# Loading w_tok in two halves, loading w_ch1 later, and a new order of the opening and the weave, in a block-sparse attention followed by a ResMLP block

## The chip, the core and the metric

The kernel runs on one core of one Trainium2 chip. That core has five engines that run side by side, each with an instruction stream of its own: PE (matrix multiply and transposes), DVE (vector), ACT (activation functions), POOL (GpSimd, elementwise work and the issue of loads) and SP (issue of transfers). Each stream is executed in order, so an instruction that waits holds up everything behind it on its engine. The metric is device microseconds (us) of one execution; lower is better.

## What is computed

```
scores = q @ k^T / 8, masked in blocks of 32 (neighbours, first and last
         block, and 3 sampled blocks a row); attn = softmax(scores)
x   = attn @ v                 # 4 batches, 8 heads of 64, 768 tokens
a1  = alpha1 * x + beta1       # heads side by side: 512 columns
u   = x + lam * (w_tok @ a1)   # w_tok: 768 x 768, mixes tokens
a2  = alpha2 * u + beta2
out = u + lam * (relu(a2 @ w_ch1) @ w_ch2)   # 512 -> 2048 -> 512
```

All inputs are float32; the work is done in bfloat16 and float16, with sums in float32.

## The kernel before

**Pairs and units.** Heads are worked in pairs: 16 pairs (4 batches of 4), pair i with heads w = 0 and 1. A pair's scores are cut into nine units, each of which is one `emit_qk` (PE, L583), one `emit_exp` (ACT, L601) and, two units later, its `emit_pv` (PE, L630 or L653), which multiplies by v and by a column of ones. When a head is complete, `emit_finish` divides on DVE (L670, L671) into x_sb, and `emit_a1pp` makes `a1pp`, the affine input of the token mixing, in two instructions (L687, L688), on POOL or, where `A1V` holds 1 (index 2i + w) or a batch ends, on DVE. `job_tok` then multiplies by the transposed w_tok (L795, six matmuls a block of 128 tokens), or, for the later pairs, `job_tok2` (L819, 12 matmuls a token T below). The result is added to x_sb and cast (L810 or L831, L837), transposed into `uT` (by PE, L846, or by a DMA, `emit_udma` and `emit_uscale`), and fed to the MLP: `job_f1` (four matmuls L884, relu L891 on ACT) and `job_f2` (L903, four matmuls a call, then an add L912 and a store).

**Two score buffers.** QK of unit u writes one of two `sp` buffers in PSUM and must wait until exp of unit u - 2 has read it.

**The opening** (the loop over `s`, 45 steps, pairs 0 to 4). Step s issues QK(s), exp(s), the jobs that `PLAN` gives it with a fraction under 0.5, PV of unit s - 2, and then the jobs with a fraction of 0.5 or more. A slot in `PLAN` is that step number. Step 2, 11, 20 and so on also issue loads that no slot has asked for yet. From step 42 (`OPEN`), `POUR[s - 42]` calls of `job_f1` come in between. In the opening the mask is part of the score (24 extra rows in `kText` and `qText`); `rows1` to `rows3` copy these rows on DVE or POOL (L439), `layv00` and `layv01` cast pair 0's v (L313), `layk01` and `layq01` cast the second head's k and q, and `tps0` transposes them and copies them out of PSUM (L471). QK(4) is the first unit that reads the second head. `bcast0` to `bcast2` spread lam, alpha1 and beta1 over the partitions (L719, L728, L730), `lv1` and so on copy a pair's v (L313), `tk` and `tq` transpose a pair's k and q on PE (L493), `mask0` to `mask17` build the mask for the later pairs on POOL (L519), `lam0` to `lam16` scale w_ch2 by lam on DVE (L765).

**Loads.** `emit_load` (L302), `emit_wtk_load` (L772), `emit_w1_load` (L753) and `emit_w2_load` (L759) are issued by POOL and share one DMA queue. The raw k and v of a pair each have two buffers, so a load waits for the copy or transposes that read the buffer two pairs ago. w_tok is one load of all its tokens; its six jobs `wt0` to `wt5` (`emit_wtok_t`) each transpose one of six interleaved columns for all 768 output tokens (six transposes, one copy), so `tok` of any block needs all six.

**The weave** (from pair 5 on) is an order written out by hand: one string for three units, `W1` for pairs 5 to 7, `W2` for 8 to 11 and again for 12 to 15, `W3` for the rest. `q` issues the three QK and the first exp, `x` a further exp, `k` the multiplication of an exp by the mask (DVE, L618), `p` the PV of one key block, `f` and `g` one call of `job_f1` and `job_f2`, `T` one `job_tok2`, `s` opens a finished pair's jobs, `d` and `v` its `emit_udma` and `emit_uscale`, `L` a load, `Q`, `K` and `Y` the next pair's q, k (DMA transposes issued by SP) and v, and `0`, `1`, `2` the slots of `PLAN` from 45 on.

**PSUM.** Besides the two `sp` buffers there are three `mm` buffers for everything else and one `op` for PV.

Of the kernel before, what the change touches and what calls it, by code (L numbers as in the profile page):

```python
# [13 lines left out]
BF = mybir.dt.bfloat16  # L14
# [6 lines left out]
S = 768  # L21
# [5 lines left out]
P = 128  # L27
NT = S // P
# [9 lines left out]
OPEN = 42  # L38
UTD = [1, 1]
TDM = [1, 0]  # L40
A1V = [1, 0, 0, 1, 0, 0, 0, 1]
POUR = [3, 1, 1]
W1 = [
# [9 lines left out]
]  # L53
W2 = [
# [12 lines left out]
]  # L67
W3 = [
# [3 lines left out]
]  # L72
WEAVE = W1 + W2 * (B - 2) + W3
ENG = {
# [16 lines left out]
    "tq1": 0,  # L91
}
PLAN = {
    "layv00": 0.29,
    "wtkl": 0.42,
    "warm1": 0.49,
    "loadv2": 0.58,
    "layk01": 1.22,
    "layq01": 1.25,
    "mask_cols": 1.5,  # L100
    "rows1": 2.08,
    "tps0": 2.52,
    "parts": 2.83,
    "mask1": 2.94,
    "w1_0": 2.96,
    "tq1": 4.55,
    "layv01": 4.3,
    "rows2": 4.5,
    "tk1": 4.82,
    "lv1": 5.01,  # L110
    "bcast0": 5.1,
    "rows3": 5.84,
    "loadk3": 6.08,
    "bcast2": 6.12,
    "loadv3": 7.02,
    "mask3": 7.41,
    "loadk2": 8.21,
    "loadq2": 8.52,
    "bcast1": 8.8,
    "loadq3": 9.23,  # L120
    "a1pp0": 9.37,
    "w1_2": 9.64,
    "w1_1": 10.3,
    "columns": 11.32,
    "wt2": 11.35,
    "wt1": 11.76,
    "wt5": 12.19,
    "lv2": 12.84,
    "wt4": 13.01,
    "wt0": 13.43,  # L130
    "loadv4": 13.94,
    "w1_3": 14.3,
    "tq2": 14.44,
    "loadq4": 14.54,
    "wt3": 15.31,
    "columns_use": 16.32,
    "tk2": 16.6,
    "tok0_0": 17.05,
    "tok0_1": 17.4,
    "tk3": 18.13,  # L140
    "loadk4": 18.23,
    "tok0_2": 20.0,
    "tq3": 20.4,
    "mask8": 20.72,
    "loadk5": 20.73,
    "mask2": 20.89,
    "tok0_3": 21.32,
    "tok0_4": 22.02,
    "lv3": 22.91,
    "mask6": 22.94,  # L150
    "mask0": 23.62,
    "tok0_5": 23.87,
    "loadq5": 24.3,
    "tok1_0": 24.53,
    "mask4": 24.64,
    "w2_0": 24.82,
    "mask7": 25.08,
    "lv4": 25.4,
    "tok1_1": 25.6,
    "tok1_2": 27.2,  # L160
    "loadv5": 27.53,
    "tok1_3": 27.74,
    "tok1_4": 28.91,
    "tok1_5": 29.7,
    "w2_2": 29.98,
    "mask5": 30.09,
    "tq4": 30.41,
    "mask15": 30.72,
    "udma0": 30.82,
    "tk4": 31.72,  # L170
    "udma1": 31.9,
    "w2_1": 32.02,
    "tq5": 32.51,
    "mask9": 32.65,
    "tok2_0": 33.91,
    "tk5": 34.64,
    "usc0": 34.69,
    "tok2_1": 34.88,
    "mask14": 34.9,
    "mask13": 35.48,  # L180
    "tok2_2": 35.71,
    "mask11": 35.79,
    "tok2_3": 36.37,
    "lam16": 37.24,
    "mask17": 37.68,
    "w2_3": 37.7,
    "mask16": 37.75,
    "tok2_4": 37.77,
    "mask10": 37.9,
    "tok3a_0": 38.34,  # L190
    "tok3a_1": 38.43,
    "tok2_5": 38.51,
    "tok3a_2": 38.52,
    "tok3a_3": 38.85,
    "tok3a_4": 39.48,
    "tok3b_0": 39.51,
    "tok3b_1": 39.52,
    "tok3b_2": 39.53,
    "tok3b_3": 39.54,
    "ut2": 39.85,  # L200
    "tok3a_5": 40.02,
    "mask12": 40.23,
    "tok3b_4": 40.23,
    "usc1": 40.28,
    "lv5": 40.42,
    "ut3_0": 40.8,
    "tok3b_5": 41.21,
    "cast3": 42.22,
    "lam2": 42.25,
    "lam3": 43.09,  # L210
    "ut3_1": 43.63,
    "lam1": 44.85,
    "lam10": 44.92,
    "lam9": 45.25,
    "lam7": 45.27,
    "lam0": 45.32,
    "lam11": 45.58,
    "lam6": 45.9,
    "lam13": 46.09,
    "lam5": 47.61,  # L220
    "lam14": 47.82,
    "lam4": 47.9,
    "lam8": 49.72,
    "lam12": 49.8,
    "lam15": 50.13,
}


# [1 line left out]
def kernel(  # L230
# [16 lines left out]
    nc = tc.nc  # L247
# [30 lines left out]
    def ptile(shape, dt, name):  # L278
        return pp.tile(shape, dt, name=name, tag=name)
# [44 lines left out]
    identb = const[:, 0:P]  # L324
# [65 lines left out]
    for o in (slice(0, 4), slice(4, NT)):  # L390
# [4 lines left out]
        out=eqt,  # L395
# [55 lines left out]
    def mm_tile(shape=(P, DM), dt=FP):  # L451
        return psum.tile(list(shape), dt, name="mm", tag="mm", bufs=3)
# [210 lines left out]
    def emit_finish(i, w):  # L663
        b, hp = i // NP, i % NP
        if (hp, w) == (0, 0):
            x_sbs[b] = ap_.tile([P, NT, DM], FP, name="x_sb", tag="x_sb", bufs=3)
        op, n = ops.pop((i, w))
        assert n == 36
        rcp = ap_.tile([P, NT], FP, name="rcp", tag="rcp", bufs=2)
        nc.vector.reciprocal(out=rcp[:], in_=op[:, :, D])  # L670
        nc.vector.tensor_tensor(  # L671
            out=x_sbs[b][:, :, ts(2 * hp + w, D)],
            in0=op[:, :, 0:D],
            in1=rcp[:].unsqueeze(2).broadcast_to([P, NT, D]),
            op=ALU.mult,
        )
# [20 lines left out]
    wtokT = ptile([P, NT, S], BF, "wtokT")  # L697
# [5 lines left out]
    parts = ptile([P, P], BF, "parts")  # L703
# [63 lines left out]
    wtks = {}  # L767

    def emit_wtk_load():
        t = ap_.tile([P, NH, QC], BF, name="hts", tag="hts", bufs=2)  # L770
        wtks[0] = t[:, 0:12, :].rearrange("p (o w) n -> p o (w n)", o=NT)
        nc.gpsimd.dma_start(wtks[0], moe_w_tok.rearrange("(p o) s -> p o s", o=NT))  # L772

    def emit_wtok_t(os_):
        wtk = wtks[0]
        tps = mm_tile((P, NT, P), BF)
        for ot in range(NT):
            nc.tensor.transpose(tps[:, ot, :], wtk[:, ot, os_:S:NT], identb[:])  # L778
        nc.vector.tensor_copy(out=wtokT[:, os_, :], in_=tps[:])

    toks = {}
    ubfs = {}
# [206 lines left out]
    for m in (32, 64):  # L991
        nc.gpsimd.tensor_tensor(
            out=pick[0:96],
# [36 lines left out]
    for i in range(1, XP):  # L1030
        tps = emit_tps if i < MP else emit_tdma if TDM[i - NP] else emit_tph
# [57 lines left out]
    for s in range(N1):  # L1089
# [108 lines left out]
```

## Time and profile before

| | |
|---|---|
| median of 3 runs | 303.16 us (302.95 to 303.28) |
| the profiled execution | 303.09 us |
| its span, first to last instruction | 301.4 us |
| granted TensorE clock, mean | 0.998 |
| PE busy | 295.3 us (98%) |
| ACT busy | 215.3 us (71%) |
| DVE busy | 193.1 us (64%) |
| POOL busy | 113.1 us (38%) |
| opening, to the weave's first QK | 0 to 58.6 us |

How to read it: a row of a view in order of time has the start in us from the span's start, the length, the engine, the line, the operation, the names of what is written and read, the shape, and how many instructions are merged in it; in brackets the idle time of the engine before it and what ended it. A row of a group has the count, then busy us, mean ns of one, and idle us before, with what ended it. Matmuls are pipelined, so one that is listed with 0.33 us may be followed by the next after 0.16; the chain of waits, which goes from end to end, shows the real spacing.

### The profile page before, as it was taken

The page shows a single profiled execution, that of the slowest core. Times are in us where ns is not written, and L with a number is a line of the kernel's source. Part 1 is how long each engine was busy: PE and PEld are TensorE (multiplying, and loading weights), DVE is VectorE, ACT ScalarE, POOL GpSimd, SP SyncE. Part 2 cuts the span into 40 slices and gives each one's busy share as a digit, 9 for nine tenths or more (in the row PEclk, how much of TensorE's full clock was granted, in tenths as well). Part 3 has the DMA queues.
Part 4 walks back from the last instruction along what each step waited for, and adds up shares of the span by engine and source line. Part 5 has one row for each costly group of instructions (what it writes and reads, how often), then busy time and mean ns, then how long its engine had stood idle before and what let it go on. Part 6 is the DMA issues. An engine that isn't in the chain of part 4 may idle for free.

```text
span 301.4 us, 7199 instructions
## 1 busy us (share of the span) xinstructions
PE 295.3 (98%) x2976; PEld 184.5 (61%) x2996; DVE 193.1 (64%) x372; ACT 215.3 (71%) x314; POOL 113.1 (38%) x150
## 2 busy tenths in 40 slices
PE   8999999999999999999999999999999999999996
PEld 3687888655567556565665556565675664555543
DVE  3998799887758899845377779854476872000012
ACT  4999997999879775889778774889868610663310
POOL 8989589344328422613408501703206300000000
PEclk9999999999999999999999999999999999999999
DMA  6999999918297697970746693880411004100011
GB/s 191 188 198 204 204 165 186 155 29 129 68 132 115 111 140 120 130 159 2 115 78 111 115 171 89 124 165 3 63 32 23 37 35 122 37 0 35 37 70 70
DMA packets 57892, 31.34 MB, mean 104 GB/s; under 512 B 37952, under 2 KB 54764, under 8 KB 57732
## 3 DMA queue, kind: packets, MB, share of 16 engines
q0 software_dynamic: 16608, 14.22, 32.1%
q1 hardware_dynamic: 40820, 16.19, 25.5%
q10 hardware_dynamic: 432, 0.48, 0.5%
q8 instruction: 23, 0.38, 0.5%
q14 instruction: 9, 0.07, 0.1%
HBM read 29.83 MB, written 6.29 MB: 120 GB/s over the span
## 4 chain that ended last, share of the span: by engine, by line
PE 94%; ACT 3%; DMA 1%; issue 1%; DVE 0%; ACTq 0%
PE mm L884 28%; PE mm L903 26%; PE sp L583 10%; PE op L653 8%; PE mm L819 8%; PE mm L583 4%; PE mm L795 3%; ACT eT L601 2%; PE op L630 2%; DMA const<-const_c 1%; PE mm L923 1%; PE mm L630 1%; PE mm L493 1%; PE mm L778 1%; ACT kTs L420 1%
## 5 line engine op out<-in xcount | busy, mean ns | idle before, releaser
L601 ACT ACTIVATE eT<-sp,expb 128x1024 f16<-128x1024 f32 x111 | 118.4, 1118 | 3.0 <-PE sp L583 2.5
L891 ACT ACTIVATE hts<-mm 128x384 bf16<-128x384 f32 x128 | 62.1, 496 | 47.9 <-PE mm L884 47.1
L884 PE MATMUL mm<-uT,w1b 128*128 128x384 bf16 x512 | 92.6, 326 | 0.0
L618 DVE TENSOR_TENSOR eT<-eT,mask 128x1024 f16<-128x1024 f16 x99 | 74.8, 779 | 26.2 <-ACT eT L601 26.0
L903 PE MATMUL mm<-w2b,hts 128*128 128x512 bf16 x348 | 85.7, 379 | 1.1
L687 POOL TENSOR_TENSOR a1pp<-x_sb,vbc 128x384 bf16<-128x384 f32 x27 | 32.7, 1211 | 123.1 <-DVE x_sb L671 118.8
L884 PEld LDWEIGHTS <-w1b 128*128 128x128 bf16 x512 | 48.1, 98 | 35.0 <-issue 3.4
L903 PEld LDWEIGHTS <-hts 128*128 128x128 bf16 x368 | 34.0, 98 | 38.7 <-issue 4.0
L601 ACT ACTIVATE eT<-mm,expb 128x512 f16<-128x512 f32 x66 | 41.8, 686 | 18.5 <-PE mm L583 18.2
L912 DVE TENSOR_TENSOR ot<-x_sb,mm 128x512 f32<-128x512 f32 x23 | 15.7, 684 | 45.4 <-PE mm L903 45.4
L653 PEld LDWEIGHTS <-eT 128*128 128x128 f16 x792 | 29.6, 98 | 8.7 <-issue 1.5
L653 PE MATMUL op<-vext,eT 128*128 128x65 f16 x792 | 31.7, 194 | 0.0
L688 POOL TENSOR_TENSOR a1pp<-a1pp,vbc 128x384 bf16<-128x384 bf16 x27 | 27.3, 1009 | 2.1
L583 PE MATMUL sp<-qTs,kTs 88*128 88x512 bf16 (+1 forms) x120 | 27.0, 326 | 0.9 <-ACT eT L601 0.7
L819 PE MATMUL mm<-a1pp,wtokT 128*128 128x256 bf16 x216 | 25.6, 273 | 0.0
L819 PEld LDWEIGHTS <-wtokT 128*128 128x128 bf16 x216 | 20.8, 98 | 4.2 <-ACT hts L891 0.8
L583 PE MATMUL sp<-qhT,khT 64*128 64x256 bf16 (+1 forms) x176 | 19.7, 322 | 0.0
L630 PEld LDWEIGHTS <-eT 128*128 128x128 f16 x360 | 15.0, 97 | 3.7
L583 PEld LDWEIGHTS <-khT 64*128 64x128 bf16 x264 | 10.5, 94 | 10.9 <-issue 6.8
L831 DVE TENSOR_TENSOR x_sb<-x_sb,mm 128x512 f32<-128x512 f32 x18 | 12.3, 685 | 7.1 <-PE mm L819 6.8
L671 DVE TENSOR_TENSOR x_sb<-op,rcp 128x384 f32<-128x384 f32 x28 | 15.6, 557 | 1.0
L837 DVE CAST ubf<-x_sb 128x256 bf16<-128x256 f32 (+1 forms) x44 | 13.7, 347 | 0.9
(92 smaller groups left out, 225.5 us busy)
## 6 DMA issues: line engine op xcount, KB each, us to landing
out_dram<-ot SPq DMA_DIRECT2D x23, 256.0 KB
qpad<-in_q_dram POOLq DMA_DIRECT2D x15, 192.0 KB, 3.8
kr<-in_k_dram POOLq DMA_DIRECT2D x15, 192.0 KB, 5.7
vr<-in_v_dram POOLq DMA_DIRECT2D x15, 192.0 KB, 6.0
w1b<-in_moe_w_ch_dram POOLq DMA_DIRECT2D x4, 512.0 KB, 10.9
w2b<-in_moe_w_ch_dram POOLq DMA_DIRECT2D x4, 512.0 KB, 6.6
hts<-in_moe_w_tok_dram POOLq DMA_DIRECT2D x1, 1152.0 KB, 10.6
x_sb<-in_k_dram ACTq DMA_DIRECT2D x2, 192.0 KB
```

Source lines behind the costliest of these rows:

```text
L583: nc.tensor.matmul(sp[jj][:, dst], lhsT, rhs, start=True, stop=True, skip_group_check=True,)
L601: nc.scalar.activation(dst, at, AF.Exp, bias=expb[:], scale=SCALE)
L618: nc.vector.tensor_mul(out=e, in0=e, in1=keep)
L630: nc.tensor.matmul(op[0][:, o, :], ets[u][:, jj, h * QB + n * P : h * QB + n * P + P], vexts[i % NVB][:, w, 2 * jp + jj, :], start=op[1] == 0,
L653: nc.tensor.matmul(op[0][:, o, :], ets[u][:, jj, h * QB + n * P : h * QB + n * P + P], vexts[i % NVB][:, w, 2 * jp + jj, :], start=op[1] == 0,
L687: eng.tensor_tensor(out=dst, in0=x_sbs[b][:, :, cols], in1=bc[0], op=ALU.mult)
L688: eng.tensor_tensor(out=dst, in0=dst, in1=bc[1], op=ALU.add)
L819: nc.tensor.matmul(ps[:, o], wtokT[:, os_, ts(2 * n + o, P)], a1pps[i][:, os_, :], start=(os_ == 0 and o == 0), stop=(os_ == NT - 1 and o ...
L884: nc.tensor.matmul(ps[:, 0:QC], w1b[:, dk, ts(n, P)], uTs[b][:, dk, ts(c, QC)], start=(dk == 0), stop=(dk == 3),)
L891: nc.scalar.activation(hts[(b, c)][:, n, :], ps[:, 0:QC], AF.Relu)
L903: nc.tensor.matmul(ps[:], ht[:, nk, ts(o % 3, P)], w2b[:, nk, :], start=(nk == 0), stop=(nk == NH - 1),)
L912: nc.vector.tensor_tensor(out=ot[:], in0=x_sbs[b][:, o, :], in1=ps[:], op=ALU.add)
```

## The change

The load of w_tok is issued as two DMAs, over the first three and the last three of the six token groups. The transposes are cut accordingly: `wt0` to `wt2` take two interleaved columns each for the first 384 output tokens, `wt3` to `wt5` for the last 384. Each still makes six transposes and one copy of 768 columns. `A1V` gives a1pp(1,0) to DVE in place of a1pp(1,1). `POUR` issues its five `f1` in steps 43 and 44 (2 and 3; a negative count is none) in place of steps 42 to 44 (3, 1, 1). `PLAN` keeps its 132 jobs and gets new slots; the loads of w_ch1 go from slots 2 to 14 to slots 31 to 41, those of w_ch2 from 24 to 37 to 4 to 26. All strings of the weave are written anew with the same kinds of tokens.

```diff
-A1V = [1, 0, 0, 1, 0, 0, 0, 1]
-POUR = [3, 1, 1]
+A1V = [1, 0, 1, 0, 0, 0, 0, 1]
+POUR = [-19, 2, 3]
 W1 = [
-    "q f Y x f 0 f p k 1 f k f p x 2 f f k f f",
-    "q L f x Q f f f k p x f p 0 k 1 p k 2",
...
+    "q f f 0 K Q 1 k x k f f 2 f p x f p k f f f",
+    "q 0 f k 1 x f s 2 f k Y p L f p x f p k",
...
 W2 = [
...
-    "q k x v 0 1 p g k x k f g f g 2",
+    "q k L p x f s x 0 g f 1 d g k g k 2",
 ]
 W3 = [
-    "p p p f g v f s g T T T g g d g g g g d g g v g v g g f f f f f f",
-    "f f f f f f f f f f f f g f f g f g f g f f g g f g f f g f f g g g f g",
-    "f f g g g g g g g g g g g g",
+    "p p p v f g s g T T T d g g d g g g g v g g g g v g f",
+    "f f f f f f f f f f f f f f f f g f g g f f g f f f f f g f f g g f f g g f g f g g f g g g g g g g g g g g",
+    "g",
 ]
...
     def emit_wtk_load():
...
-        nc.gpsimd.dma_start(wtks[0], moe_w_tok.rearrange("(p o) s -> p o s", o=NT))
-
-    def emit_wtok_t(os_):
-        wtk = wtks[0]
-        tps = mm_tile((P, NT, P), BF)
-        for ot in range(NT):
-            nc.tensor.transpose(tps[:, ot, :], wtk[:, ot, os_:S:NT], identb[:])
-        nc.vector.tensor_copy(out=wtokT[:, os_, :], in_=tps[:])
+        src = moe_w_tok.rearrange("(p o) s -> p o s", o=NT)
+        for o in (slice(0, 3), slice(3, NT)):
+            nc.gpsimd.dma_start(wtks[0][:, o], src[:, o])
+
+    def emit_wtok_t(n):
+        h, o2 = divmod(n, 3)
+        tps = mm_tile((P, 2, 3, P), BF)
+        for os_ in range(2):
+            for ot in range(3):
+                nc.tensor.transpose(
+                    tps[:, os_, ot, :],
+                    wtks[0][:, 3 * h + ot, 2 * o2 + os_ : S : NT],
+                    identb[:],
+                )
+        nc.vector.tensor_copy(
+            out=wtokT[:, 2 * o2 : 2 * o2 + 2, ts(h, 3 * P)],
+            in_=tps[:].rearrange("p s o q -> p s (o q)"),
+        )
```

The slots of `PLAN` that the prediction goes through, before and after (a job that both orders give nearly the same slot is left out):

| job | before | after | job | before | after |
|---|---|---|---|---|---|
| rows1 | 2.08 | 0 | wt0 | 13.43 | 9.72 |
| rows2 | 4.5 | 0.25 | wt1 | 11.76 | 10.69 |
| rows3 | 5.84 | 2.34 | wt2 | 11.35 | 11.71 |
| parts | 2.83 | 0.58 | wt3 | 15.31 | 13.91 |
| layk01, layq01 | 1.22, 1.25 | 0.57, 0.97 | wt4, wt5 | 13.01, 12.19 | 12.55, 14.01 |
| layv01 | 4.3 | 1.18 | tok0_0, tok0_1 | 17.05, 17.4 | 15.06, 16.15 |
| mask_cols | 1.5 | 2.21 | tok0_2 to tok0_5 | 20.0 to 23.87 | 18.84 to 20.64 |
| lv1 | 5.01 | 8.08 | tok1_0 | 24.53 | 23.37 |
| tk1 | 4.82 | 5.86 | tok2_0 | 33.91 | 32.44 |
| bcast1 | 8.8 | 7.12 | tok2_3, tok2_4 | 36.37, 37.77 | 34.23, 34.66 |
| a1pp0 (pair 0, w = 0) | 9.37 | 9.12 | w1_0 to w1_2 | 2.96, 10.3, 9.64 | 31.69, 31.86, 32.16 |
| loadv3, loadq3 | 7.02, 9.23 | 8.39, 9.3 | w1_3 | 14.3 | 41.14 |
| columns | 11.32 | 6.44 | w2_0, w2_2 | 24.82, 29.98 | 4.38, 10.56 |
| udma0, udma1 | 30.82, 31.9 | 23.87, 33.68 | w2_1, w2_3 | 32.02, 37.7 | 26.5, 19.2 |
| lam11, lam1 | 45.58, 44.85 | 31.28, 41.96 | mask9, mask16, mask4 | 32.65, 37.75, 24.64 | 42.79, 43.78, 44.8 |

More of the change, by code (lines that the diff above doesn't have):

```diff
@@ L93 @@
 PLAN = {
[L94 to L116, printed above, removed]
+    "rows1": 0,
+    "wtkl": 0,
@@ L117 @@
+    "warm1": 0.05,
+    "rows2": 0.25,
+    "layv00": 0.33,
+    "layk01": 0.57,
+    "parts": 0.58,
+    "loadv2": 0.69,
+    "layq01": 0.97,
+    "layv01": 1.18,
+    "mask_cols": 2.21,
+    "rows3": 2.34,
+    "tps0": 2.54,
+    "w2_0": 4.38,
+    "tq1": 4.69,
+    "mask1": 4.79,
+    "tk1": 5.86,
+    "bcast0": 6.33,
+    "columns": 6.44,
+    "mask13": 6.77,
+    "bcast2": 6.8,
+    "bcast1": 7.12,
+    "loadk3": 7.4,
+    "lv1": 8.08,
     "loadk2": 8.21,
+    "loadv3": 8.39,
     "loadq2": 8.52,
-    "bcast1": 8.8,
@@ L120 @@
[L120 to L225, printed above, removed]
+    "a1pp0": 9.12,
+    "loadq3": 9.3,
+    "wt0": 9.72,
+    "w2_2": 10.56,
+    "wt1": 10.69,
+    "mask3": 11.65,
+    "wt2": 11.71,
+    "columns_use": 11.82,
+    "wt4": 12.55,
+    "wt3": 13.91,
+    "wt5": 14.01,
+    "lv2": 14.19,
+    "mask7": 14.61,
+    "tq2": 14.81,
+    "tok0_0": 15.06,
+    "mask2": 15.17,
@@ new lines @@
+    "tk2": 15.31,
+    "tok0_1": 16.15,
+    "loadq4": 16.26,
+    "loadv4": 17.03,
+    "lam16": 18.04,
+    "tok0_3": 18.84,
+    "mask11": 18.86,
+    "tok0_4": 19,
+    "loadk4": 19.16,
+    "w2_3": 19.2,
+    "tok0_2": 19.94,
+    "tok0_5": 20.64,
+    "tk3": 21.8,
+    "tq3": 22.41,
+    "loadk5": 23.18,
+    "loadq5": 23.25,
+    "tok1_0": 23.37,
+    "lv4": 23.87,
+    "udma0": 23.87,
+    "loadv5": 24.12,
+    "tok1_1": 24.86,
+    "tok1_3": 25.03,
+    "mask5": 25.65,
+    "tok1_2": 25.72,
@@ new lines @@
+    "mask6": 26.43,
+    "w2_1": 26.5,
+    "lv3": 26.86,
+    "tq4": 27.5,
+    "tok1_4": 28.17,
+    "mask12": 28.96,
+    "tok1_5": 29.1,
+    "tk4": 29.97,
+    "tk5": 31.1,
+    "lam11": 31.28,
+    "w1_0": 31.69,
+    "w1_1": 31.86,
+    "tq5": 32.1,
+    "w1_2": 32.16,
+    "tok2_0": 32.44,
+    "mask10": 32.62,
+    "mask0": 32.9,
+    "udma1": 33.68,
+    "mask8": 33.83,
+    "tok2_1": 33.98,
+    "tok2_3": 34.23,
+    "tok2_2": 34.28,
+    "tok2_4": 34.66,
+    "mask14": 34.97,
+    "usc0": 35.74,
@@ new lines @@
+    "tok2_5": 36.33,
+    "tok3a_0": 37.57,
+    "lv5": 37.82,
+    "tok3a_1": 38.2,
+    "tok3a_3": 38.61,
+    "tok3a_4": 38.99,
+    "mask15": 39.06,
+    "tok3a_2": 39.11,
+    "usc1": 39.2,
+    "tok3b_0": 40.23,
+    "tok3b_1": 40.45,
+    "mask17": 40.56,
+    "tok3b_2": 40.84,
+    "ut2": 40.84,
+    "w1_3": 41.14,
+    "tok3b_3": 41.4,
+    "lam1": 41.96,
+    "ut3_0": 42.13,
+    "tok3a_5": 42.58,
+    "mask9": 42.79,
+    "tok3b_4": 42.83,
+    "lam6": 43.53,
+    "tok3b_5": 43.69,
+    "mask16": 43.78,
@@ L226 @@
+    "lam2": 44.05,
+    "lam0": 44.24,
+    "cast3": 44.34,
+    "lam14": 44.61,
+    "ut3_1": 44.67,
+    "mask4": 44.8,
+    "lam12": 45.15,
+    "lam9": 45.67,
+    "lam5": 45.94,
+    "lam4": 46.02,
+    "lam15": 46.27,
+    "lam7": 48.55,
+    "lam8": 48.9,
+    "lam10": 48.92,
+    "lam3": 49.98,
+    "lam13": 51.07,
 }
```

36 rows, old and new, of tables (W1, W2) are left out of this document.

## The prediction, made before the changed kernel was run

> **What bounds the kernel now.** I read the page's span first, then PE's groups in the weave, the chain of waits, and then each engine's order of time in the opening. The two largest groups of PE from 58.6 us to the end (line, shapes, count | busy, mean | idle before):
>
> ```profile
> L884 PE MATMUL mm<-uT,w1b 128*128 128x384 bf16 x492 | 88.9, 326 | 0.0
> L903 PE MATMUL mm<-w2b,hts 128*128 128x512 bf16 x348 | 85.7, 379 | 1.1
> ```
>
> PE never waits there (348 of L903's 368 matmuls are in the records, so its 1.1 is holes in them; the smaller groups show 0.0). The diff neither adds nor removes a matmul, so four fifths of the span cannot become shorter; they can only get a stall. What can be won lies in the opening. Its chain of waits (start, length, what), and ACT's first row of exponentials in order of time:
>
> ```profile
> 15.53 2.25 ACT eT L601 x2
> 17.82 0.60 PE sp L583 x4
> 18.42 0.67 PE mm L778 x12
> 19.09 0.43 PE sp L583 x2
> 19.53 0.34 PE mm L778 x6
> 19.86 0.49 PE op L630 x16
> ...
> 28.07 0.59 PE sp L583 x4
> ...
> 34.34 0.59 PE sp L583 x2
> ```
> ```profile
> 7.36 14.64 ACT L601 ACTIVATE eT<-sp,expb 128x1024 f16<-128x1024 f32 x14
> ```
>
> Up to 17.8 us the chain runs through the exponentials, afterwards through PE. ACT does one step in 14.64/14 = 1.046 us. After 17.8 no piece of ACT is on the chain; PE waits there only at 28.07 and 34.34, where QK takes 0.59 instead of 0.44. So the kernel is PE's work plus PE's idle time in the opening, and each us of that idle time is one of the span.
>
> The chain also gives PE's own prices: six 128-wide matmuls (transposes, or one `tok` job) 0.34, one 128-wide 0.056, QK 0.44, sixteen PV matmuls 0.49 (0.03 each).
>
> **Step 4 gets later.** DVE's and PE's order of time:
>
> ```profile
> 7.68 0.45 DVE L313 CAST vext<-x_sb 128x384 f16<-128x384 f32 x1
> ...
> 9.02 0.54 DVE L439 COPY kTs<-kTs 24x768 bf16<-24x768 bf16 x1
> 9.59 0.29 DVE L471 COPY kTs<-mm 64x256 bf16<-64x256 bf16 x1
> 9.91 0.28 DVE L471 COPY qTs<-mm 64x256 bf16<-64x256 bf16 x1
> ```
> ```profile
> 10.54 0.60 PE L583 MATMUL sp<-qTs,kTs 88*128 88x256 bf16 x4
> ...
> 13.69 0.60 PE L583 MATMUL sp<-qTs,kTs 88*128 88x256 bf16 x4
> 14.70 0.59 PE L583 MATMUL sp<-qTs,kTs 88*128 88x512 bf16 x2 [0.41 <-ACT eT L601]
> ...
> 17.14 0.41 PE L630 MATMUL mm<-vext,eT 128*128 128x65 f16 x8
> 17.82 0.60 PE L583 MATMUL sp<-qTs,kTs 88*128 88x256 bf16 x4 [0.28 <-ACT eT L601]
> ```
>
> The two copies at 9.59 and 9.91 feed QK(4). The change puts `layv01` (a cast like the one at 7.68, 0.45) and `rows3` (a copy like the one at 9.02, 0.57 to the next start) ahead of them, 1.0 us in all; `rows1` only moves among the others. The copies then end at 11.2, QK(4) starts at 11.25 instead of 10.54 and ends at 11.85. exp(4) is due at 7.36 + 4 x 1.046 = 11.54. **PE loses 0.70, ACT 0.35.**
>
> **PE's two waits are filled.** Before, PE was through with step 7 at 13.69 + 0.44 = 14.13 and waited 0.57 for exp to free a score buffer; before QK(11) it was done at 17.14 + 8 x 0.03 = 17.39 and waited 0.43. After the change `bcast1` (4 x 0.056 = 0.22) stands ahead of QK(8), so PE arrives at 14.13 + 0.70 + 0.22 = 15.05, and the gate opens at 14.70 + 0.35 = 15.05. Ahead of QK(11) `wt0` and `wt1` (0.68) are new and `bcast1` is gone: 15.05 + 2.69 - 0.22 + 0.68 = 18.20, gate 18.17. At QK(11) the clock is 0.38 later and 0.68 more work is done: **0.30 won**. By step 18 both orders have done the same jobs. Between steps 18 and 36 the new order has two `tok` jobs more (tok2_3, tok2_4: 0.68), and the waits at 28.07 and 34.34 (0.15 each) go: **0.30 more**. The five `f1` of POUR shift by a step, number and price unchanged.
>
> **The split load is what allows wt0 that early.** The loads' issue on POOL, their landing:
>
> ```profile
> 6.05 0.72 POOL L302 DMA_DIRECT2D vr<-in_v_dram  x1
> ...
> 7.38 0.58 POOL L772 DMA_DIRECT2D hts<-in_moe_w_tok_dram  x1
> ```
> ```profile
> vr<-in_v_dram POOLq DMA_DIRECT2D x1, 192.0 KB, 6.0
> ```
> ```profile
> hts<-in_moe_w_tok_dram POOLq DMA_DIRECT2D x1, 1152.0 KB, 10.6
> ```
>
> v of pair 1 lands at 12.0, w_tok at 18.0: 1152 KB in 5.9 us behind it. Half of it lands at about 15.0. PE comes to wt0 after QK(8), 20 PV, QK(9) and 8 PV: 15.05 + 0.44 + 0.6 + 0.44 + 0.25 = 16.8, so 1.8 us hide the load. The second issue costs POOL 0.58, which delays `parts` and v2, both with us to spare. The second half's first user, wt3, comes at step 13, near 21.
>
> **POOL's queue is the tight place.** `lv1` goes from slot 5 to 8, and POOL's load v3 needs the buffer that it frees:
>
> ```profile
> 13.97 0.43 DVE L313 COPY vext<-vr 128x768 f16<-128x768 f16 x1
> 14.43 0.69 DVE L728 COPY vbc<-mm 128x512 f32<-128x512 f32 x1
> ...
> 16.57 0.56 DVE L671 TENSOR_TENSOR x_sb<-op,rcp 128x384 f32<-128x384 f32 x1
> ```
> ```profile
> 17.81 1.00 POOL L687 TENSOR_TENSOR a1pp<-x_sb,vbc 128x384 bf16<-128x384 f32 x1 [1.17 <-DVE vbc L730]
> 18.89 0.92 POOL L688 TENSOR_TENSOR a1pp<-a1pp,vbc 128x384 bf16<-128x384 bf16 x1
> ```
>
> lv1 stood at 13.97; the copies' 1.0 less `layv01` (0.45) shift it to 14.5, and three broadcasts (0.65 each) and a finish (0.7) now precede it: it ends at about 17.6. Behind it on POOL: v3 (0.72), a1pp(0,0) (1.94), q3 (0.72), a1pp(0,1) (2.0): done at 23.0. The job tok0_0 that reads it moves from slot 17 to 15, where PE comes to it after five QK (2.2), five jobs of six transposes (1.7) and 36 PV (1.1) from 18.2: at about 23.2. QK(16) is queued behind. Likewise A1V takes a1pp(1,1) from DVE to POOL (and (1,0) to DVE), and tok1_0, its reader, comes a slot (1.05) earlier; I count no slack there either. I take 0.1 for both together, since the first has 0.2 to spare by the sum; bounds 0 (both in time) and 0.76 (below).
>
> [...]
>
> ```profile
> L687 POOL TENSOR_TENSOR a1pp<-x_sb,vbc x27: 989/1304/1382, 17.8 to 237.6; 128x384 bf16<-128x384 f32 x27
> ```
>
> The first instruction of the pair takes 1.00 in the opening, where DVE mostly copies out of PSUM, and 1.38 at its longest; a pair stretched alike would cost 1.38 x 1.94 = 2.7. The sum takes 1.94; what 2.7 would do is the third rival.
>
> **What hides the rest.** The w_ch1 loads leave the early queue, and w2_0 and w2_2, as large, take two of their places. w1_3, issued last, is the one that could be late:
>
> ```profile
> 44.91 0.99 POOL L687 TENSOR_TENSOR a1pp<-x_sb,vbc 128x384 bf16<-128x384 f32 x1 [1.03 <-DVE x_sb L671]
> ```
> ```profile
> w1b<-in_moe_w_ch_dram POOLq DMA_DIRECT2D x4, 512.0 KB, 10.9
> ```
>
> After that pair (1.9) come four masks, three loads (0.72 each) and w1_3 on POOL, so it is issued at about 51 and lands by 62. Its first user, the eighth `f` of the weave's first string, comes near 64. Without these 2 us PE would lose one for one. The masks are 18 short POOL copies as before; three of them now stand behind a1pp(4,0), which starts when step 42's PV is done, and the first k that needs them comes in the weave's first string, behind the five `f1` of steps 43 and 44 and two more. Of the other moved jobs, `columns` and the `udma` give SP small loads and two transposes that nobody reads within a step; the `lam` jobs only move on DVE, which before and after has work waiting on PE there; SP's K and Q of pair 6 go out a whole pair (three strings) before their QK.
>
> **The weave costs nothing by its order**, as far as its strings can be read against prices:
>
> ```profile
> L618 DVE TENSOR_TENSOR eT<-eT,mask 128x1024 f16<-128x1024 f16 x99 | 74.8, 779 | 26.2 <-ACT eT L601 26.0
> ```
>
> Two places become nearer. At the end of W2 the last k (0.78) is followed by "2 p p p" instead of "f g f g 2 p p p"; two p, 24 x 0.03 = 0.72 us of PV, hide it, and its x stands far ahead. In W3 the first T stands behind "v f g s g" after the third p instead of "f g v f s g": the finish and a1pp on DVE are hidden by one `f`, 4 x 88.9/492 = 0.7, and two `g`, 8 x 85.7/348 = 2.0, where one `f` more stood before. Without cover the first place would cost 0.1, the second 0.7, the `f` that is missing.
>
> **The sum.** 0.30 + 0.30 - 0.10 = 0.5 us won; in the profiled execution (303.09 us round a span of 301.4) 302.6. The median of the runs is 0.07 higher, so 302.65, and I name 302.6.
>
> **Rivals.**
> *No early loss.* If DVE reaches the two copies at 9.6 as before (its casts overlap: the two at 8.05 take 0.81), PE keeps the 0.70 but the gates stay where they were, and only the work moved ahead of them is won: 0.68 + 0.30 = 1.0, 302.1. Against it: DVE shows no gap from 7.68 to 10.2.
> *The halves don't come apart.* If the DMA engines serve both together, the first half lands at 17.9 too and wt0, queued on PE ahead of QK(10), waits 1.0: 303.16 - 0.5 + 1.0 = 303.7. For it: both are issued within 0.6 us. Against it: loads issued one behind the other have landed one behind the other.
> *Slower: POOL's a1pp pairs gate PE.* If a pair takes 2.7, a1pp(0,1) ends at 23.0 + 2 x 0.76 = 24.5 and PE stands 1.3 us at tok0_0; at tok1_0 a pair of 2.7 costs another 0.7. Together 2.0 less the 0.6 won: 304.5. It decides from a pair of about 2.3 us on: 0.6 lost at the first place and 0.3 at the second pass the gain. For it: no slack at either place. Against it: at 17.81 and 18.89 the pair took 1.94 beside a busy DVE.
>
> **How the numbers follow.** A difference under 0.2% (0.6 us: below 302.55 or above 303.77) is none that I could tell. Forecast 0.46, with a range of its own from 302.2 to 303.0 and 0.26 of it below 302.55; no early loss 0.18; halves together 0.12; POOL's pairs, or a stall of that size, 0.24. So faster 0.26 + 0.18 = 0.44, the same 0.20 + 0.12 = 0.32, slower 0.24. The range is 301.9 to 304.5: from 0.2 under the first rival to the third.
>
> **What would show it.** Right: QK(4) at 11.2 and exp(4) near 11.9; no ACT bracket before QK(8) and QK(11); the first half of w_tok landed by 15.2; wt0 near 16.8; tok0_0 near 23.2 without an idle bracket on PE or PEld; the weave's first QK (58.6 before) near 58.1; 0.0 idle in its groups. Wrong: PE idle at tok0_0 or tok1_0 with POOL's a1pp as releaser (third rival), PE idle at wt0 with the DMA as releaser (second), or any idle time of PE after 58 us, which no step above contains.

## The result, and the profile after

The changed kernel takes **302.50 us** (median of 23 runs, 302.17 to 304.02), the kernel before 303.16 in the same comparison (23 runs). The ratio is 0.9976, with a 95% interval of 0.9969 to 0.9984: 0.66 us, or 0.24%, faster. The forecast was 302.6.

The one execution that was profiled is the longest of the 23, 304.02 us round a span of 302.3, so its profile shows something that most executions don't have; a second profile of the same kernel, taken later and called "again" below (302.83 round 301.1), stands beside it. First PE's waits, in all, number and longest; the changed kernel's first profile, where the warm-up's 0.8 and one of 0.2 at the start are left out:

```profile
PE mm L781 <- DMA hts<-in_moe_w_tok_dram: 0.9, 1, 0.9
...
PE sp L583 <- ACT eT L601: 0.4, 1, 0.4
PE mm L481 <- DMA const<-const_c: 0.4, 1, 0.4
PE sp L583 <- DVE qTs L471: 0.4, 1, 0.4
```

and the second profile, with all that it lists:

```profile
PE op L463 <- PEq L1190: 0.8, 1, 0.8
PE sp L583 <- DVE qTs L471: 0.4, 1, 0.4
PE sp L583 <- ACT eT L601: 0.3, 1, 0.3
```

The waits before QK(8) and QK(11) are gone from both. What is left is step 4's wait for the copies, one at QK(2) for the first exponential, behind which no exponential comes late, and, in the first profile alone, 0.4 for const and 0.9 us at `wt0` for the load of w_tok. PE's order of time in the first profile (start, length, what):

```profile
11.41 0.38 PE L583 MATMUL sp<-qTs,kTs 88*128 88x256 bf16 x2 [0.35 <-DVE qTs L471]
...
15.09 0.59 PE L583 MATMUL sp<-qTs,kTs 88*128 88x512 bf16 x2
...
16.58 0.41 PE L630 MATMUL mm<-vext,eT 128*128 128x65 f16 x8
17.90 0.54 PE L781 MATMUL mm<-const,hts 128*128 128x128 bf16 x6 [0.91 <-DMA hts<-in_moe_w_tok_dram]
...
59.19 0.39 PE L583 MATMUL mm<-qhT,khT 64*128 64x512 bf16 x2
```

and in the second:

```profile
11.16 0.38 PE L583 MATMUL sp<-qTs,kTs 88*128 88x256 bf16 x2 [0.45 <-DVE qTs L471]
...
14.84 0.59 PE L583 MATMUL sp<-qTs,kTs 88*128 88x512 bf16 x2
...
16.59 0.52 PE L781 MATMUL mm<-const,hts 128*128 128x128 bf16 x6
...
23.25 0.49 PE L803 MATMUL mm<-a1pp,wtokT 128*128 128x128 bf16 x6
...
57.99 0.39 PE L583 MATMUL mm<-qhT,khT 64*128 64x512 bf16 x2
```

The load of the first half, from issue to landing, in the first profile and in the second (KB, us):

```profile
hts<-in_moe_w_tok_dram POOLq DMA_DIRECT2D x1, 576.0 KB, 9.9
```
```profile
hts<-in_moe_w_tok_dram POOLq DMA_DIRECT2D x1, 576.0 KB, 6.0
```

Issued at 7.99 it landed at 17.9; issued at 8.20, at 14.2. PE was ready for `wt0` at 16.58 + 8 x 0.03 = 16.82 in the first case, so it lost 17.90 - 16.82 = 1.08.

The weave, from the page of the second profile, has no idle time in its large groups:

```profile
L892 PE MATMUL mm<-uT,w1b 128*128 128x384 bf16 x512 | 93.6, 326 | 0.0
...
L911 PE MATMUL mm<-w2b,hts 128*128 128x512 bf16 x368 | 87.4, 379 | 0.0
```

This table puts the profiles beside each other. "Opening" is from the first exponential to the weave's first QK, "end" from the last matmul to the end of the span. From the weave's first QK to the last matmul it is 239.75 to 239.77 in every one of them.

| kernel | this execution, us | first exponential | weave's first QK | opening | end |
|---|---|---|---|---|---|
| before | 303.09 | 7.36 | 58.61 | 51.25 | 2.99 |
| before, second profile | 303.20 | 7.09 | 58.73 | 51.64 | 3.01 |
| changed | 304.02 | 7.47 | 59.19 | 51.72 | 3.37 |
| changed, second profile | 302.83 | 7.04 | 57.99 | 50.95 | 3.36 |

The first profile's 304.02 adds up from it: the weave starts 0.58 later than before (0.11 from the start, 1.08 at `wt0`, less 0.61 won), and the end is 0.38 longer. An ordinary execution of 302.5 has 1.7 us outside the span as all have, so its weave starts at 302.5 - 1.7 - 3.36 - 239.77 = 57.7, against 58.6 to 58.7 before. So **the weave starts about 1.0 us earlier, twice what was forecast, and the end gave back 0.37, which was not forecast at all.** The experiments are about these two, and about the terms in between.

### The profile page after: what moved, and what is told of

Its sections match the earlier page's. It is cut to its first block, busy times and chain, and to the rows that moved or that the text cites. A ratio compares the mean times of both kernels' runs of the same rounds, so it can differ in the third digit from the quotient of the medians.

```text
span 302.3 us, 7186 instructions
## 1 busy us (share of the span) xinstructions
PE 294.4 (97%) x2972; PEld 183.6 (61%) x2996; DVE 192.7 (64%) x372; ACT 214.4 (71%) x314; POOL 116.6 (39%) x151
## 4 chain that ended last, share of the span: by engine, by line
PE 92%; DMA 4%; POOL 1%; issue 1%; DVE 0%; POOLq 0%
PE mm L892 28%; PE mm L911 26%; PE sp L583 10%; PE op L653 8%; PE mm L827 8%; PE mm L583 4%; DMA hts<-in_moe_w_tok_dram 3%; PE mm L803 3%; PE op L630 2%; PE mm L630 1%; PE mm L931 1%; DMA x_sb<-in_q_dram 1%; PE mm L781 1%; PE mm L493 1%; POOL qpad L302 0%
## 5 line engine op out<-in xcount | busy, mean ns | idle before, releaser
L892 PE MATMUL mm<-uT,w1b 128*128 128x384 bf16 x512 | 93.6, 326 | 0.1
L899 ACT ACTIVATE hts<-mm 128x384 bf16<-128x384 f32 x128 | 61.4, 495 | 45.2 <-PE mm L892 43.7
L618 DVE TENSOR_TENSOR eT<-eT,mask 128x1024 f16<-128x1024 f16 x99 | 76.3, 785 | 22.5 <-ACT eT L601 22.0
L911 PE MATMUL mm<-w2b,hts 128*128 128x512 bf16 x344 | 84.6, 379 | 1.1
L653 PEld LDWEIGHTS <-eT 128*128 128x128 f16 x792 | 30.3, 98 | 9.6 <-issue 2.9
L653 PE MATMUL op<-vext,eT 128*128 128x65 f16 x792 | 32.9, 194 | 0.0
L688 POOL TENSOR_TENSOR a1pp<-a1pp,vbc 128x384 bf16<-128x384 bf16 x27 | 30.1, 1114 | 2.1
L583 PEld LDWEIGHTS <-khT 64*128 64x128 bf16 x264 | 10.3, 94 | 12.5 <-issue 8.7
L630 PEld LDWEIGHTS <-eT 128*128 128x128 f16 x360 | 15.1, 97 | 4.3
```

The lines of the kernel that those rows point to most:

```text
L583: nc.tensor.matmul(sp[jj][:, dst], lhsT, rhs, start=True, stop=True, skip_group_check=True,)
L618: nc.vector.tensor_mul(out=e, in0=e, in1=keep)
L630: nc.tensor.matmul(op[0][:, o, :], ets[u][:, jj, h * QB + n * P : h * QB + n * P + P], vexts[i % NVB][:, w, 2 * jp + jj, :], start=op[1] == 0,
L653: nc.tensor.matmul(op[0][:, o, :], ets[u][:, jj, h * QB + n * P : h * QB + n * P + P], vexts[i % NVB][:, w, 2 * jp + jj, :], start=op[1] == 0,
L688: eng.tensor_tensor(out=dst, in0=dst, in1=bc[1], op=ALU.add)
L892: nc.tensor.matmul(ps[:, 0:QC], w1b[:, dk, ts(n, P)], uTs[b][:, dk, ts(c, QC)], start=(dk == 0), stop=(dk == 3),)
```

## The experiments

Each kernel ran in turns with the kernel before on its chip; the kernel before took 303.25 to 303.33 there, the changed kernel 302.48. Times are medians.

### again: the changed kernel a second time

> The changed kernel once more, unaltered, for a profile of an ordinary execution. Theory (the 0.91 us that wt0 waited for w_tok's first half belong to the slow execution that was profiled): the median stays at 302.5; in a profile of 302.2 to 302.8 the first half has landed by 16.8, wt0 shows no idle time with the DMA as releaser, and the weave's first QK stands at 58.0 to 58.3. Rival (the wait is in every execution, and the slow one lost its time elsewhere): wt0 waits 0.6 to 1.1 us in this profile too, the first QK of the weave is near 59, and the difference to 304.0 lies behind the weave.

Measured: 302.48 (302.14 to 305.9, 12 runs). The profile is the one above: landed at 14.2, no idle time at `wt0`, the weave at 57.99. So the wait for w_tok is not in every execution. That it makes the slow ones is shown for the one at 304.02; the others above 303.4 have no profile (of 35 runs of this kernel four, and at the one of 305.9 the granted clock was 0.989).

### one_load: w_tok by one DMA

```diff
-        for o in (slice(0, 3), slice(3, NT)):
-            nc.gpsimd.dma_start(wtks[0][:, o], src[:, o])
+        nc.gpsimd.dma_start(wtks[0], src)
```

> The changed kernel with w_tok loaded by one DMA again; the transposes and their order stay. Theory (the split load is what allows wt0 at 16.8): all of w_tok lands at 17.9 to 20 us, wt0 waits for it 1.0 to 2.5 us on PE ahead of QK(10), and the time is 303.3 to 304.5: the gain is gone. Rival (the halves land together anyway, or ACT's lead takes up the wait): within 0.2 us of the changed kernel, 302.3 to 302.7.

Measured: 304.36 (303.12 to 307.0), 1.9 more than the changed kernel. In the profiled execution, one of the shortest (303.34), PE's order of time shows:

```profile
17.15 0.54 PE L780 MATMUL mm<-const,hts 128*128 128x128 bf16 x6 [0.91 <-DMA hts<-in_moe_w_tok_dram]
```

The new order asks for w_tok at about 16.2 here, and the whole load landed at 16.9 to 17.9 in the four profiles that have one. The split is what pays for `wt0` to `wt2` in the places of PE's old waits, as expected. This profile shows 0.91 of the 1.9; the longer executions have no profile.

### split_in_old: the halves alone, in the old order

The kernel before, with the diff's `emit_wtk_load` and `emit_wtok_t`.

> The kernel before, in its old order, with w_tok loaded and transposed in two halves. Theory (the split alone moves nothing: in the old order every transpose of w_tok comes after 18 us, when all of w_tok has landed): within 0.2 us of the kernel before, 303.0 to 303.4. Rival (the halves themselves gain, through half a load that stands less in the way of v, q and k of pair 2): 302.5 to 302.9. Other rival (the second issue of 0.58 us on POOL costs): 303.5 or more.

Measured: 303.61, ratio 1.0017 (1.0000 to 1.0034): by its median the second rival, though the interval begins at no difference. PE's order of time:

```profile
12.72 0.38 PE L719 MATMUL mm<-parts,pick 96*128 96x128 bf16 x4 [0.70 <-POOL parts L714]
```

This is not a cost of the load as such. In the old order POOL does `parts` behind w_tok and the three loads of pair 2; the second issue makes it 0.6 later, and the first broadcast, `bcast0`, waits for it. The profile of before had shown no such wait, so the next two runs asked whether the kernel before has it in other executions.

### before_again: the kernel before, a second profile

> The kernel before once more, unaltered, for a second profile. In the profile of before the first exponential stood at 7.36, behind a wait of 0.96 us of DVE for const; in five other executions const landed earlier. Theory (the landing of const is chance, and an early start is partly lost in the old order, because bcast0 then waits for parts, which POOL does behind v, q and k of pair 2): exp(0) between 6.6 and 7.0, PE idle 0.1 to 0.4 us at the first broadcast with POOL's parts as releaser, the weave's first QK at 58.1 to 58.5. Rival (the start belongs to the kernel): exp(0) at 7.3 to 7.4 again and no wait at the broadcast.

Measured: 303.20. The first exponential stood at 7.09 (0.1 outside the forecast range), PE waited 0.29, and ACT 0.30 behind it; the weave started at 58.73, a little later than expected. PE, POOL and ACT in order of time:

```profile
12.50 0.38 PE L719 MATMUL mm<-parts,pick 96*128 96x128 bf16 x4 [0.29 <-POOL parts L714]
```
```profile
12.03 0.42 POOL L714 TENSOR_TENSOR parts<-rest,part 12x128 bf16<-12x128 f32 x1
```
```profile
13.66 8.48 ACT L601 ACTIVATE eT<-sp,expb 128x1024 f16<-128x1024 f32 x8 [0.30 <-PE sp L583]
```

The execution that the prediction was made from was one where const, a small load, landed late, and its first exponential came at 7.36. DVE, POOL and PE there:

```profile
5.07 0.22 DVE L394 TENSOR_TENSOR const<-sampi,const 24x72 f32<-24x72 int32 x1 [0.96 <-DMA const<-const_c]
```
```profile
11.61 0.42 POOL L714 TENSOR_TENSOR parts<-rest,part 12x128 bf16<-12x128 f32 x1
```
```profile
12.32 0.39 PE L719 MATMUL mm<-parts,pick 96*128 96x128 bf16 x4
```

`parts` was ready at 12.03, 0.29 ahead of the broadcast, and no wait shows. In the second profile PE is through with QK(5) 0.28 earlier, and `parts` ends 0.42 later (12.45), because POOL itself runs later there; the two together make the wait. Where the start is earlier, the old order keeps PE back at `parts`, whose end hangs on POOL and not on the first exponential: split_in_old had its first exponential at 6.60, and its weave began at 58.97 all the same.

### parts_first: the kernel before with parts ahead of pair 2's loads

```diff
-    "parts": 2.83,
+    "parts": 0.5,
```

> The kernel before with one edit: parts on POOL ahead of the loads of pair 2 (slot 0 instead of 2), as the change has it. Theory (the early place of parts is a part of the gain that the prediction left out): 0.15 to 0.5 us faster than the kernel before, 302.8 to 303.1, and no idle time at the first broadcast. Rival (the broadcast never waited in an ordinary execution): within 0.15 us of the kernel before.

Measured: 303.03 (302.52 to 305.53) against 303.27; the interval of the ratio is 0.9980 to 1.0015, which does not decide. Five of its twelve runs, 302.52 to 302.81, lie below the kernel before's lowest of 303.00 in 23, so an execution can win 0.5; the others don't. In its profile the broadcast does not wait, the weave starts at 58.30 after a first exponential at 6.81, and a first transposition of w_tok now waits about 0.2 us for the whole load, landed at 17.87. `parts` alone moves PE on to the next thing that is late; the split takes that away too.

### no_early: layv01 and rows3 behind tps0's copies again

```diff
-    "layv01": 1.18,
-    "rows3": 2.34,
+    "layv01": 4.3,
+    "rows3": 5.84,
```

> The changed kernel with layv01 and rows3 behind tps0's copies again, as before the change (slots 4 and 5). Theory (they cost PE 0.70 us and ACT 0.35 us at step 4): QK(4) back at 10.5 to 10.7, exp(4) without a wait, PE waits about 0.3 us ahead of QK(8) and not at QK(11), and 0.35 us are won: 302.1 to 302.2. Rival (PE's wait ahead of QK(8) and QK(11) swallows all of it, or w_tok's first half now comes too late for a PE that is earlier): the same as the changed kernel within 0.15 us.

Measured: **302.07** (301.88 to 302.33), ratio to before 0.9955 (0.9939 to 0.9972): 0.41 less than the changed kernel, 0.35 forecast. ACT and PE in order of time:

```profile
6.64 13.40 ACT L601 ACTIVATE eT<-sp,expb 128x1024 f16<-128x1024 f32 x13
```
```profile
13.81 0.40 PE L719 MATMUL mm<-parts,pick 96*128 96x128 bf16 x4 [0.32 <-DVE kTs L499]
```

Thirteen exponentials follow each other without a wait. PE stands 0.32 us ahead of QK(8), as long as expected, though at `bcast1`, which waits for DVE to empty a buffer. The early place of the two pieces is a loss that the change carries.

### pool_tail: eight instructions more at the end of POOL's program

```diff
+    for _ in range(8):
+        nc.gpsimd.memset(gate[:], 0.0)
```

> The changed kernel with eight small memsets more at the end of POOL's program, of a value that nobody reads. In all profiles with the new strings the end behind the last matmul takes 3.33 to 3.43 us, with the old ones 2.98: POOL takes 0.39 instead of 0.08 us between two instructions of the closing barrier, and an instruction packet arrives there that arrived at 227 us before. Theory (the change left POOL so few instructions behind a border of its code that the next block is fetched only at the end): the end takes 3.0 us, and the time is 302.1 to 302.25, 0.3 less than the changed kernel. Rival (the end is longer for another reason, of the last store or of SP): 302.4 to 302.6 and 3.3 us at the end.

Measured: **302.07** (301.86 to 302.26), ratio to before 0.9957 (0.9943 to 0.9971), and 3.00 us at the end. The closing barrier's line in "again", on POOL and on ACT (instructions, length in ns, first and last start), and the last 2.7 us of DMA there:

```profile
L1201 POOLq EVENT_SEMAPHORE  x4: 17/17/17, 300.0 to 301.0; - x4
...
L1201 ACTq EVENT_SEMAPHORE  x2: 17/17/17, 300.5 to 301.1; - x2
```
```profile
q14 instruction: 1, 0.01, 0.8%
```

In pool_tail the same line shows:

```profile
L1203 POOLq EVENT_SEMAPHORE  x4: 17/17/17, 299.6 to 300.3; - x4
...
L1203 ACTq EVENT_SEMAPHORE  x2: 17/17/17, 299.8 to 300.3; - x2
```

From POOL's first semaphore of the barrier to ACT's it takes 0.5 us in "again" and 0.2 here. The instruction packet that came at 301.1, with the end of the span, comes at 218 in pool_tail and at 227 in the kernel before. So the change's 0.37 us at the end hangs on how many instructions POOL's program has: with eight more, which do nothing, the kernel is 0.4 faster. The traces of all fourteen profiles agree: with 203 or more POOL instructions (waits included; 204 before, 210 here) the end takes 2.98 to 3.01, with 201 or 202 (202 after) 3.33 to 3.43. That POOL waits there for code is a guess that the trace does not bear out by itself: the packet comes at 301.1, more than 0.5 us behind the slow step of the barrier.

### wtok_first: the first half ahead of v of pair 1

```diff
-    emit_load(1)
+    emit_load(1, "qk")
+    emit_wtk_load(0)
+    emit_load(1, "v")
```

> The changed kernel with w_tok's first half issued on POOL ahead of v of pair 1 instead of behind it and the three small jobs. Theory (the first half, landed at 14.2 to 17.9 so far against a need at 16.6, has too little cover in some executions): it lands at 11.5 to 13.5, no execution stands 0.9 us above the median any more unless its clock was lower, and the median stays within 0.1 us of 302.5; v of pair 1 lands near 13 to 15, ahead of lv1 at 16.3 to 17.3. Rival (v of pair 1 becomes late, and with it v of pair 3 and the a1pp pairs on POOL): 0.3 us or more slower, with idle time at lv1 or at the first tok.

Measured: 302.34 (302.01 to 302.58), 0.14 less than "again" and 0.16 under the 302.5 that was forecast within 0.1. The first half, issued 1.9 us earlier than there (6.33), landed at 14.2, no earlier than there, so that part of the forecast failed. From the change's own place it landed anywhere from 14.1 to 17.9 in seven profiles, so one landing does not say whether the early place moves the middle of that spread. v of pair 1 landed at 15.2, in time. None of ten executions is long, but none of no_early's six, pool_tail's eight and pool_pair's eleven is either, with the load in the change's place; whether the early place helps stays open.

### pool_pair: a1pp(0,1) 1.1 us longer on POOL

```diff
-        eng.tensor_tensor(out=dst, in0=x_sbs[b][:, :, cols], in1=bc[0], op=ALU.mult)
+        for _ in range(2 if (i, w) == (0, 1) else 1):
+            eng.tensor_tensor(
+                out=dst, in0=x_sbs[b][:, :, cols], in1=bc[0], op=ALU.mult
+            )
```

> The changed kernel with the first instruction of a1pp(0,1) done twice on POOL, about 1.1 us more between a1pp(0,0) and tok0_0. Theory (tok0_0 has no slack: PE stands 0.15 us there in every profile of the changed kernel, just behind the end of a1pp(0,1)): PE waits 1.1 to 1.3 us at tok0_0 with a1pp as releaser and the time is 303.3 to 303.7. Rival (the 0.15 us are something else, and POOL has room): less than 0.3 us of wait and a time within 0.2 us of the changed kernel.

Measured: 303.04 (302.66 to 303.33), 0.56 more than the changed kernel. PE's order of time:

```profile
23.74 0.49 PE L806 MATMUL mm<-a1pp,wtokT 128*128 128x128 bf16 x6 [1.04 <-POOL a1pp L691]
```

The wait came in full, and the opening is 51.97, 1.02 more than in "again". That the time rose by only 0.56 is the end: 2.99 instead of 3.36, because this edit happens to add one instruction to POOL's program, and one is enough. tok0_0 has no slack, as theory had it.

### early_and_tail, all_four: what gained, put together

The first has the edits of no_early and pool_tail. The second has wtok_first's as well, and

```diff
-    "loadq3": 9.3,
+    "loadq3": 10.57,
```

> The changed kernel with the two edits that each gained on their own: layv01 and rows3 behind tps0's copies, and eight small memsets more at the end of POOL's program. Theory (the two have nothing to do with each other: 0.41 and 0.41 us): 301.6 to 301.75, 3.0 us at the end, exp(4) without a wait. Rival (part of either gain was the chip's chance or the same thing twice): 301.9 to 302.2.

> The same two edits, w_tok's first half ahead of v of pair 1, and the load q3 behind a1pp(0,1) on POOL instead of ahead of it. Theory (the first half has cover again although PE is earlier, and the 0.15 us at tok0_0 go): 301.4 to 301.6, no excess at tok0_0, no execution 0.9 us above the median unless its clock was lower. Rival (v of pair 1, now later, or q3 takes the place of what was removed): 301.6 or more, with a wait at lv1, at v3 on POOL or at tq3.

Measured: 301.89 (301.59 to 303.53; ratio to before 0.9961, 0.9949 to 0.9972) and 301.93 (301.73 to 302.31; 0.9956, 0.9943 to 0.9969). Both are 1.3 to 1.4 us faster than the kernel before and 0.6 faster than the changed one, and both miss their forecasts (301.75 and 301.6 at most): the two gains add up for the most part (0.59 of 0.41 + 0.41). What the missing 0.2 went to wasn't settled. all_four has no excess at tok0_0 in its profile, yet is no faster. The load q3, issued behind a1pp(0,1) at 23.18, takes 7.3 us, and PE's weights for `tq3` wait for it, the place that the expectation's rival named:

```profile
30.55 0.34 PEld L493 LDWEIGHTS <-qpad 128*128 128x128 bf16 x6 [0.24 <-DMA qpad<-in_q_dram]
```

QK(22) is done at 29.99 + 0.44 = 30.43, so PE loses 0.12 here: most of the 0.15 won at tok0_0 is lost again seven steps later. The profiled execution of early_and_tail is its longest, 303.53, and shows the chance in the start:

```profile
5.50 0.80 PE L481 MATMUL mm<-const,qk 128*128 128x128 bf16 x6 [0.66 <-DMA const<-const_c]
```

### w_swap: w_ch1 early again, in w_ch2's places

```diff
-    "w2_0": 4.38,
+    "w1_0": 4.38,
...
-    "lam11": 31.28,
+    "lam11": 41.9,
```

> The changed kernel with the four loads of w_ch1 in the places of w_ch2's four, in slots 4, 10, 19 and 26, and w_ch2's at 31.7, 31.9, 32.2 and 33.9; lam11, which needs a part of w_ch2, goes from slot 31 to 41. Theory (loading w_ch1 late is worth nothing of itself: it only lets w_ch2's loads, of the same 512 KB, take its places, and every one lands long before its first user): 302.35 to 302.65, the same opening and the weave's length of 239.77. Rival (the later w_ch1 is a part of the gain): 302.8 or more. Other rival (w_ch1 issued at 51 us is a small loss at the weave's first f, which this takes away): 302.2 or less.

Measured: 303.71 (303.24 to 306.69), 1.2 more than the changed kernel; the expectation failed, and the time is one that the first rival named. Its profiled execution (304.62) has two waits; DVE's and PE's order of time:

```profile
56.93 0.62 DVE L765 TENSOR_TENSOR w2b<-w2b,lam_bcb 128x512 bf16<-128x512 bf16 x1 [1.73 <-DMA w2b<-in_moe_w_ch_dram]
57.48 0.54 DVE L818 TENSOR_TENSOR x_sb<-x_sb,mm 128x384 f32<-128x384 f32 x1
```
```profile
17.63 0.54 PE L781 MATMUL mm<-const,hts 128*128 128x128 bf16 x6 [1.35 <-DMA hts<-in_moe_w_tok_dram]
...
58.07 0.81 PE L892 MATMUL mm<-uT,w1b 128*128 128x384 bf16 x4 [0.54 <-DVE x_sb L818]
```

The first half of w_tok is late again, in this execution. The new wait is DVE's: the `lam` jobs scale w_ch2 at 53 to 60 us, its last load lands only at 56.9, and the x_sb addition queued behind the waiting job holds PE for 0.54. So a late w_ch2 costs: its first user is a job on DVE, and PE waits behind that job. This is not the whole 1.2, though: even the shortest execution, 303.24, is 1.1 above the changed kernel's shortest, and what the rest is stays open, as no ordinary execution was profiled. The run does not say what a late w_ch1 is worth by itself.

## Why the prediction was right, and where it was not

**The weave** was costed at nothing, and it is: 239.76 before, 239.77 after.

**Step 4** was right in place and size. QK(4) was forecast 3.89 after the first exponential, exp(4) some 4.5; in "again" the second half of QK(4) starts 11.16 - 7.04 = 4.12 after it and exp(4) 4.53:

```profile
7.04 4.13 ACT L601 ACTIVATE eT<-sp,expb 128x1024 f16<-128x1024 f32 x4
11.57 9.24 ACT L601 ACTIVATE eT<-sp,expb 128x1024 f16<-128x1024 f32 x9 [0.40 <-PE sp L583]
```

no_early gave back 0.41 for the 0.35 named. The rival "no early loss" fell with that. The price of the two pieces was read from rows where POOL did not copy beside them. Here one of the two stretches beside POOL's `rows2`, `rows3` in "again":

```profile
8.92 0.34 DVE L313 CAST vext<-x_sb 128x384 f16<-128x384 f32 x1
...
9.44 1.03 DVE L439 COPY kTs<-kTs 24x768 bf16<-24x768 bf16 x1
```
```profile
9.43 0.82 POOL L439 COPY kTs<-kTs 24x768 bf16<-24x768 bf16 x1
```

In the first profile it is `layv01` that takes 0.99 beside that copy, and `rows3` takes 0.35.

**PE's two waits** are filled: none is left before QK(8) and QK(11). How much of the sum came of it can be read from QK's places. These are QK(18) and QK(36) in the profile of before, and then in "again":

```profile
26.21 0.60 PE L583 MATMUL sp<-qTs,kTs 88*128 88x512 bf16 x2
...
45.28 0.60 PE L583 MATMUL sp<-qTs,kTs 88*128 88x512 bf16 x2
```
```profile
25.91 0.59 PE L583 MATMUL sp<-qTs,kTs 88*128 88x512 bf16 x2
...
45.36 0.60 PE L583 MATMUL sp<-qTs,kTs 88*128 88x512 bf16 x2
```

Counted from the first exponential (7.36 and 7.04), QK(11) comes 0.46 later with 0.68 more work done: 0.22 won, 0.30 forecast. QK(18), where both have done the same, comes at 18.85 and 18.87: nothing of it is left. Of the 0.22, 0.15 went at tok0_0, and where the rest went was not found. QK(36) comes 0.40 later with the two `tok` jobs done, 0.68: 0.28 won from step 18 on, 0.30 forecast, and no wait is left in the places of 28.07 and 34.34. So "again" won 0.3 in the opening against the execution that the prediction was made from. In pool_tail it is 0.4 (6.73 to 57.59, against 51.25), and in the first profile the 0.61 above, with the wait at `wt0` taken off: the forecast 0.5 lies among them.

**The split load** carries `wt0`, as one_load shows (1.9 us). PE came to `wt0` at 16.6 to 16.8, as forecast. The landing "at about 15.0" was right as a middle, but the spread was not in the sum: 14.1 to 16.0 in five profiles with the load in the change's place (again, no_early, pool_tail, pool_pair, early_and_tail), 17.9 in the first profile and 17.6 in w_swap. There the second rival's price (1.0) was met with 1.08, though its mechanism was not: the halves came 2.1 us apart, and both were late.

**POOL's queue** was called the tight place, and is: a1pp(0,1) was forecast to end at 23.0, and in "again" POOL's next instruction starts at 23.14, `tok0_0` at 23.25 with 0.15 of excess for the 0.1 taken. The pair took 1.94, not the third rival's 2.7:

```profile
21.18 1.02 POOL L687 TENSOR_TENSOR a1pp<-x_sb,vbc 128x384 bf16<-128x384 f32 x1
22.28 0.92 POOL L688 TENSOR_TENSOR a1pp<-a1pp,vbc 128x384 bf16<-128x384 bf16 x1
```

So that rival did not happen, but its price was right: 1.1 us more on POOL made PE wait 1.04. The stretch stayed a matter of the weave (shortest, median and longest in ns, first profile of the changed kernel):

```profile
L687 POOL TENSOR_TENSOR a1pp<-x_sb,vbc x27: 987/1296/1474, 18.7 to 238.5; 128x384 bf16<-128x384 f32 x27
```

Beside the opening's 1.02 DVE copies out of PSUM (`wtokT<-mm` in "again", 0.56 at 21.51). In the weave of the first profile one of the two longest, 1.47 at 142.67, stands beside a mask multiplication of DVE (L618, 0.69 from 142.59), and its pair took 2.8; at 94.98 the instruction took 0.99 beside another, which itself took 1.50 (L618 from 95.02). What stretches the one or the other is not shown by any run.

**The later w_ch1**: w1_3 was issued at 51.5 and landed by 60.8 (forecast 51 and 62), and no `f` waited.

**Two terms were missing from the sum.** One is in the step "The second issue costs POOL 0.58, which delays `parts` and v2, both with us to spare". In the new order that holds. But the sum gave nothing for `parts` leaving its old place, and there it had 0.29 to spare in the profile of before and was 0.40 late in the second one (ready at 12.45, while PE was done with QK(5) at 11.61 + 0.44). At like starts (the second profiles, 7.09 and 7.04) the opening won 0.69. Of this, 0.39 is what the wait behind `parts` costs the old order (openings of 51.64 and 51.25), and 0.30 is left for the forecast's 0.5. The other 0.3 of the ordinary gain is, by the profiles, that an early start now reaches the weave (pool_tail: first exponential 6.73, weave 57.59), where the old order lost it at `parts`; how often a start is early wasn't measured, and parts_first, the run on `parts` alone, did not decide, so this share is argued and not shown. The second missing term is the end: the sum takes what was won off the time of the kernel before and has no term for what follows the last matmul, and this grew by 0.37. By this count the moved work gave 0.3, `parts` and the start 0.7 that the sum did not have, and the end took 0.37. So 302.6 was met in part by luck: 0.5 forecast, 1.0 less 0.37 found.

## What to carry to other kernels

Before costing a move at nothing, look in the profile of before for how much the moved job had to spare in its old place, not only in the new one; here 0.3 us to spare in one execution was a wait of 0.3 in the next. One profile is one draw: here small loads at the start moved the first exponential between 6.53 and 7.77 among the profiles, and the wait that mattered was hidden in the draw that was read. When a wait is filled with work that reads a load, the load's spread from execution to execution, and not its median, is the cover to count; here w_tok's first half landed anywhere from 14.1 to 17.9 us.

## What of the hardware was not expected

**A few POOL instructions more or less change the end of the span, and the place of an instruction packet changes with it.** One instruction packet of 8 KB arrived at 227 us before, at the very end after, and at 218 with eight more POOL instructions; the end took 2.99, 3.36 and 3.00 us. One instruction more was enough (pool_pair: no instruction packet from 298.5 to 301.2 us, end 2.99). Of the two instruction queues in the profiles of before and after, one moved 23 packets of 16 KB (0.38 MB), this one 9 of 8 KB (0.07 MB); what the packet holds, and why the end is longer where it comes last, no run shows. Two kernels that differ by eight POOL instructions so differed by 0.4 us (302.48 and 302.07) for a reason that is in neither's algorithm, and a comparison at the level of 0.1% has to look at it.

**The same load takes 6 to 10 us.** w_tok's first half, 576 KB from the same instruction, took 6.0 us in one execution and 9.9 in another of the same kernel. Issued 1.9 us earlier than in the first of these it took 7.9 and landed no earlier.
